# The first blocks redone: x and weights on one load queue in order of use, their four layer norms in a fixed order, transposes in half banks

## The chip, the cores and the metric

The kernel runs on one core of one Trainium2 chip. The metric is the device time of one execution in microseconds (us), lower is better. The kernel before took 1696.49 us, the median of 3 runs (1696.45 to 1697.39). Every run quoted here was in the fast state (the granted clock of the TensorE over the whole span was 0.998 to 1.0) and gave a correct result.

## The reference, cut to what matters

Four layers work on a 2048 x 1024 activation `x`. A linear attention block and a gated feed-forward block alternate, each behind a layer norm. Only the first attention block matters here, and of it only the start: normalise `x`, multiply by the key columns of `wqkv`, apply `phi`.

```python
def _layernorm(x, axis=-1, eps=1e-5):
    m = jnp.mean(x, axis=axis, keepdims=True)
    v = jnp.var(x, axis=axis, keepdims=True)
    return (x - m) / jnp.sqrt(v + eps)
# attention: S = 2048, D = 1024, 32 heads
    qkv = (x @ wqkv)...                       # cut: reshape into heads
    phi = lambda t: jnp.where(t > 0, t + 1, jnp.exp(t)) + 1e-6
    pq, pk = phi(q), phi(k)
    kv = jnp.einsum("bhsd,bhse->bhde", pk, v)
    # ... cut: num / den, @ wo
x = x + attention(_layernorm(x), wqkv, wo)
x = x + feed_forward(_layernorm(x), W_gate, W_up, W_down)
# ... and both once more
```

## The kernel before

`x` is cut into 16 blocks of 128 rows, x0 to x15. For each block VectorE takes statistics of its two halves (`bn_stats`), ScalarE makes the reciprocal deviation, VectorE scales, the matrix engine (PE) transposes eight 128x128 tiles into PSUM, and VectorE or ScalarE copies them back. Four blocks make one 512-column operand. With it PE computes k0 (the first half of the keys), then k1, v0 and v1. GpSimd (POOL) casts each block into the resident float32 copy of `x`. The parts that the change touches:

```python
        ident_f = self.xnp.tile([P, P], F32, tag="xn")
        make_identity(nc, ident_f[:, :])                      # GpSimd, float32
        self.ident = self.const.tile([P, P], BF16, name="ident")
        nc.vector.tensor_copy(out=self.ident, in_=ident_f)    # VectorE cast
# ... cut
    def ln_norm(self, layer, t):
        src = self.xin.pop(t) if layer == 0 else self.x[t]
        # ... cut: bn_stats of 2 halves, bn_aggr, Ln and Exp on ScalarE -> rstd
        nc.vector.tensor_scalar(out=xn, in0=src, scalar1=mv[:, 0:1], scalar2=rstd[:, 0:1],
                                op0=ALU.subtract, op1=ALU.mult)
        if layer == 0:
            nc.gpsimd.tensor_copy(out=self.x[t], in_=src)
            if t + 3 < self.ST:
                self.load_x(t + 3)
        return xn

    def ln_turn(self, layer, t, xn):
        # ... cut
        tp = self.pst.tile([P, self.KT, P], BF16, tag="tr")   # one PSUM buffer
        for kt in range(self.KT):
            nc.tensor.transpose(tp[:, kt, :], xn[:, kt * P:(kt + 1) * P], self.ident)
        # ... cut: one copy of the whole tile, VectorE and ScalarE in turn

    def load_x(self, t):
        xin = self.xio.tile([P, self.D], BF16, tag="xio")     # three buffers
        self.nc.scalar.dma_start(out=xin, in_=self.x_v[:, t, :])
        self.xin[t] = xin
# ... cut: layer_A
        ring.free_before((l, "k0"))       # seven weight tiles of 1 MB, on nc.sync
        for q in range(self.NQ):
            if l == 0 and q == 0:
                for j in range(QT):
                    self.ln_turn(l, j, self.ln_norm(l, j))
            if q + 1 < self.NQ:
                self.ln_later(l, q + 1, 2, 4, 2)
# ... cut: run
        for t in range(3):
            self.load_x(t)
        self.layer_A(0, 1)
```

There are three buffers for arriving blocks, so x3 is asked for only when x0 has been scaled and cast. And the scheduler of the kernel language decides, when the program is built and from its own estimates of times, in which order each engine gets its instructions. On the chip every engine then follows that order.

## Time and profile before

| | before |
|---|---|
| median of runs | 1696.49 us |
| span of the profiled run | 1694.7 us |
| PE busy | 1675.2 us, 99% of the span |
| first transposes start | 11.58 us |
| fifth block's transposes end, next matmuls start | 25.81 us |
| PE busy in the 25.81 us before that | 11.51 us |

From the page of the kernel before: the span, the busy times, and the chain of waits by engine.

```profile
span 1694.7 us, 19592 instructions
...
PE 1675.2 (99%) x8304; PEld 778.6 (46%) x8304; DVE 595.0 (35%) x1002; ACT 392.5 (23%) x723; POOL 21.2 (1%) x54
...
PE 95%; DVE 3%; ACT 1%; DMA 1%; issue 0%; DVEq 0%; ACTq 0%
```

The table of windows of the kernel before follows. The columns are the window, its length, then busy time and number of instructions for each engine, the granted PE clock, the DMA share and GB/s.

```profile
core 0: us, PE busy (x) PEld busy (x) DVE busy (x) ACT busy (x) POOL busy (x), PEclk, DMA share, GB/s
0.00:25.81 25.81, 11.51 (x73) 6.53 (x74) 15.24 (x37) 7.79 (x19) 7.53 (x20) 1.00 1.00 327
25.81:50.00 24.19, 24.19 (x151) 12.52 (x149) 17.62 (x37) 11.25 (x27) 6.60 (x9) 1.00 0.28 86
50.00:1691.00 1641.00, 1639.07 (x8085) 759.58 (x8084) 561.41 (x927) 373.49 (x679) 7.11 (x25) 1.00 0.36 117
```

PE is idle for 14.3 us in the first window (25.81 − 11.51), for nothing in the second, and for under 2 us in the other 1641 us. A change to the first blocks can earn something only in the first window, and what it earns there it keeps, because everything later is bound by PE.

The timeline of PE in the kernel before is next: start, duration, engine, line, operation, output<-inputs, count, and in brackets the idle time in front and what ended it. `tp` are transposes, `ps` matmuls.

```profile
11.58 1.01 PE L153 MATMUL tp<-ident,xn 128*128 128x128 bf16 x8 [11.58 <-DVE ident L109]
13.38 1.01 PE L153 MATMUL tp<-ident,xn 128*128 128x128 bf16 x8 [0.78 <-DVE xnT L157]
14.19 2.74 PE L229 MATMUL ps<-t,xnT 128*128 128x512 bf16 x6
16.75 0.62 PE L153 MATMUL tp<-ident,xn 128*128 128x128 bf16 x8
...
20.60 0.61 PE L153 MATMUL tp<-ident,xn 128*128 128x128 bf16 x8 [1.94 <-DVE xnT L157]
21.04 4.48 PE L229 MATMUL ps<-t,xnT 128*128 128x512 bf16 x20
25.36 0.61 PE L153 MATMUL tp<-ident,xn 128*128 128x128 bf16 x8
```

Three causes of the slow head show here. PE cannot start before 11.58 us. It waits again before 13.38 and 20.60 for copies of transposed blocks. And its first six matmuls are 427 ns apart (2.74 us for six, with the pipeline's end counted in), where the 20 at 21.04 are 216 ns apart. Below, the clock of PE is called closed, or cold, while matmuls run at this half rate, and open afterwards. At the later rate the five blocks and the 32 matmuls ahead of 25.81 need 32 x 0.216 + 5 x 0.44 = 9.1 us.

The timeline of VectorE in the kernel before, the same columns, cut to the steps that feed PE:

```profile
4.61 1.29 DVE L130 BATCH_NORM_STATS2 stats<-xin 128x6 f32<-128x512 bf16 x2 [3.09 <-DMA xin<-in_A_x_dram]
7.68 0.69 DVE L130 BATCH_NORM_STATS2 stats<-xin 128x6 f32<-128x512 bf16 x1 [1.78 <-DMA xin<-in_A_x_dram]
8.29 0.19 DVE L132 BATCH_NORM_AGGREGATE mv<-stats 128x2 f32<-128x12 f32 x1
...
9.08 1.06 DVE L137 TENSOR_SCALAR xn<-xin,mv,rstd 128x1024 bf16<-128x1024 bf16 x1
...
11.32 0.20 DVE L109 CAST ident<-ident_f 128x128 bf16<-128x128 f32 x1
...
16.54 1.29 DVE L130 BATCH_NORM_STATS2 stats<-xin 128x6 f32<-128x512 bf16 x2 [2.75 <-DMA xin<-in_A_x_dram]
...
19.40 0.55 DVE L137 TENSOR_SCALAR xn<-xin,mv,rstd 128x1024 bf16<-128x1024 bf16 x1
```

x0's statistics are taken at 4.61, as soon as x0 lands. But the built order puts a statistic of x1 in front of x0's aggregate, and x1 lands at 7.68. So x0 is scaled only at 9.08. The cast of the identity, which the first transpose needs too, comes at 11.32. x3 was asked for at 10.68 us, once x0's buffer was free, and VectorE waits 2.75 us for it at 16.54.

### The profile page before, as it was taken

The numbers are of one execution on the slowest core, as the hardware profiler recorded it, in microseconds if no ns is written. First come the engines' busy times: TensorE is split into PE (matmuls) and PEld (weight loads), VectorE is DVE, ScalarE is ACT, GpSimd is POOL, SyncE is SP. The second block draws the span as 40 slices with busy tenths as digits, with TensorE's granted clock in tenths as the row PEclk, the third lists the DMA queues.
The fourth block names the chain that finished last, engine by engine and source line by source line (L and its number), as shares of the span: only waits on it lengthen the run. The fifth ranks groups of instructions, "written<-read, shape, count | busy, mean of one in ns | idle before, by whom it ended". The sixth has DMA issues, their size and how long they took to land.

```text
span 1694.7 us, 19592 instructions
## 1 busy us (share of the span) xinstructions
PE 1675.2 (99%) x8304; PEld 778.6 (46%) x8304; DVE 595.0 (35%) x1002; ACT 392.5 (23%) x723; POOL 21.2 (1%) x54
## 2 busy tenths in 40 slices
PE   6999999999999999999999999999999999999999
PEld 3554444444444444444455544444444444444444
DVE  7445994312321231232144279832112202211211
ACT  3436641210220120022033374412002101100110
POOL 3100000000000000000000000000000000000000
PEclk9999999999999999999999999999999999999999
DMA  7103011455445444444510220134554464455441
GB/s 242 32 26 125 0 51 52 145 157 169 149 134 164 151 142 156 149 149 134 182 58 1 71 80 1 50 100 140 165 182 145 130 196 135 140 180 177 146 144 34
DMA packets 198489, 202.60 MB, mean 120 GB/s; under 512 B 3840, under 2 KB 196352, under 8 KB 198400
## 3 DMA queue, kind: packets, MB, share of 16 engines
q1 hardware_dynamic: 191488, 192.95, 35.4%
q10 hardware_dynamic: 6912, 8.39, 1.5%
q8 instruction: 65, 1.06, 0.3%
q14 instruction: 24, 0.20, 0.0%
HBM read 197.13 MB, written 4.19 MB: 119 GB/s over the span
## 4 chain that ended last, share of the span: by engine, by line
PE 95%; DVE 3%; ACT 1%; DMA 1%; issue 0%; DVEq 0%; ACTq 0%
PE acc L380 23%; PE pg L363 23%; PE pu L363 23%; PE ps L229 13%; PE ps L298 5%; PE ps L311 5%; PE tp L153 2%; PE kv L204 1%; PE ps L269 1%; DMA xin<-in_A_x_dram 1%; DVE stats L130 1%; DVE x L315 0%; DVE xn L137 0%; DVE pq L273 0%; ACT r L271 0%
## 5 line engine op out<-in xcount | busy, mean ns | idle before, releaser
L363 PEld LDWEIGHTS <-t 128*128 128x128 bf16 x3584 | 349.5, 98 | 416.3
L363 PE MATMUL pg<-xnT,t 128*128 128x512 bf16 x1792 | 423.3, 379 | 0.0
L363 PE MATMUL pu<-xnT,t 128*128 128x512 bf16 x1792 | 423.3, 379 | 0.0
L380 PE MATMUL acc<-t,hT 128*128 128x512 bf16 x1792 | 388.1, 379 | 0.0
L369 DVE TENSOR_TENSOR hT<-pu,rg 128x512 bf16<-128x512 f32 x224 | 154.9, 692 | 586.0 <-PE pu L363 586.0
L368 ACT ACTIVATE rg<-pg 128x512 f32<-128x512 f32 x224 | 133.3, 595 | 891.5 <-PE pg L363 891.4
L380 PEld LDWEIGHTS <-hT 128*128 128x128 bf16 x1792 | 175.3, 98 | 211.4
L229 PE MATMUL ps<-t,xnT 128*128 128x512 bf16 x1024 | 230.4, 380 | 0.0
L229 PEld LDWEIGHTS <-xnT 128*128 128x128 bf16 x1024 | 98.5, 98 | 109.9 <-issue 1.1
L298 PE MATMUL ps<-xnT,t 128*128 128x512 bf16 x512 | 121.6, 379 | 0.2
L311 PE MATMUL ps<-T,pq 128*128 128x512 bf16 x512 | 113.4, 379 | 0.0
L174 ACT ACTIVATE e<-ps 128x512 f32<-128x512 f32 x128 | 76.2, 595 | 137.1 <-PE ps L229 116.4
L391 DVE TENSOR_TENSOR xo<-x,acc 128x512 bf16<-128x512 f32 x32 | 22.0, 688 | 171.1 <-PE acc L380 167.5
L388 DVE TENSOR_TENSOR x<-x,acc 128x512 f32<-128x512 f32 x32 | 22.0, 688 | 159.4 <-PE acc L380 157.9
L311 PEld LDWEIGHTS <-pq 128*128 128x128 bf16 x512 | 50.0, 98 | 58.5
L298 PEld LDWEIGHTS <-t 128*128 128x128 bf16 x512 | 49.7, 98 | 56.1 <-issue 1.7
L175 DVE TENSOR_SCALAR e<-e 128x512 f32<-128x512 f32 x128 | 54.9, 429 | 57.3 <-ACT e L174 56.3
L130 DVE BATCH_NORM_STATS2 stats<-x 128x6 f32<-128x512 f32 x96 | 65.4, 691 | 2.4
L153 PE MATMUL tp<-ident,xn 128*128 128x128 bf16 x512 | 39.8, 222 | 14.3 <-DVE ident L109 11.6
L235 ACT ACTIVATE pkv<-ps 128x512 bf16<-128x512 f32 x64 | 38.2, 597 | 66.2 <-PE ps L229 66.2
L153 PEld LDWEIGHTS <-xn 128*128 128x128 bf16 x512 | 34.7, 99 | 29.5 <-DVE xn L137 12.0
L315 DVE TENSOR_TENSOR x<-x,ps 128x512 f32<-128x512 f32 x64 | 43.2, 675 | 12.5 <-PE ps L311 12.0
(41 smaller groups left out, 517.8 us busy)
## 6 DMA issues: line engine op xcount, KB each, us to landing
t<-in_B_W_gate_dram SPq DMA_DIRECT2D x56, 1024.0 KB, 5.4
t<-in_B_W_up_dram SPq DMA_DIRECT2D x56, 1024.0 KB, 5.2
t<-in_B_W_down_dram SPq DMA_DIRECT2D x64, 896.0 KB, 5.8
t<-in_A_wqkv_dram SPq DMA_DIRECT2D x12, 1024.0 KB, 5.6
xin<-in_A_x_dram ACTq DMA_DIRECT2D x16, 256.0 KB, 3.6
t<-in_A_wo_dram SPq DMA_DIRECT2D x4, 1024.0 KB, 5.2
out_dram<-xo ACTq DMA_DIRECT2D x32, 128.0 KB, 3.0
```

What stands on the lines that cost most here:

```text
L130: nc.vector.bn_stats(out=stats[:, c, :], in_=src[:, c * fmax:(c + 1) * fmax])
L153: nc.tensor.transpose(tp[:, kt, :], xn[:, kt * P:(kt + 1) * P], self.ident)
L174: nc.scalar.activation(out=e, in_=ps, func=ACT.Exp)
L175: nc.vector.tensor_scalar(out=e, in0=e, scalar1=1.0, scalar2=1e-6, op0=ALU.min, op1=ALU.add)
L229: nc.tensor.matmul(ps, lhsT=self.xnT[l, q][:, kt, j * P:(j + 1) * P], rhs=w[:, kt, :], start=(kt == 0), stop=(kt == KT - 1))
L298: nc.tensor.matmul(ps, lhsT=w[:, kt, (g % 4) * P:(g % 4 + 1) * P], rhs=self.xnT[l, sc][:, kt, :], start=(kt == 0), stop=(kt == KT - 1))
L311: nc.tensor.matmul(ps, lhsT=pq[sc, g // 4][:, g % 4, j * P:(j + 1) * P], rhs=T[g // 2][:, g % 2, n2 * NW:(n2 + 1) * NW], start=(g == 0), s ...
L315: nc.vector.tensor_tensor(out=xs, in0=xs, in1=ps, op=ALU.add)
L363: nc.tensor.matmul(ps, lhsT=w[:, kt, fi * P:(fi + 1) * P], rhs=self.xnT[l, q][:, kt, :], start=(kt == 0), stop=(kt == KT - 1))
L368: nc.scalar.activation(out=rg, in_=pg, func=ACT.Relu)
L369: nc.vector.tensor_tensor(out=h[:, fi, :], in0=pu, in1=rg, op=ALU.mult)
L380: nc.tensor.matmul(acc[j], lhsT=hT[ft // 4][:, ft % 4, j * P:(j + 1) * P], rhs=wd[:, k, :], start=(ft == 0), stop=(ft == self.FT - 1))
```

## The change

The intent is to start PE earlier: bring x0 first, then the weights k0, then x1 to x3, and so on, each when it is needed, all on one queue; give x0 to x3 buffers of their own, so that x3 need not wait for x0's; fix the order of VectorE's and ScalarE's work for the first four blocks; split each block's transposes into two half banks, one copied by VectorE and one by ScalarE; make the identity in bf16 at once; and delay the casts of x0 to x3. The core of the diff:

```diff
-        ident_f = self.xnp.tile([P, P], F32, tag="xn")
-        make_identity(nc, ident_f[:, :])
         self.ident = self.const.tile([P, P], BF16, name="ident")
-        nc.vector.tensor_copy(out=self.ident, in_=ident_f)
+        make_identity(nc, self.ident[:, :])
 ... cut: ln_norm split into ln_stat (one half), ln_rstd and ln_scale
+    def head(self):
+        xh = [self.slab.tile([P, 2, self.D], BF16, tag="slab", name=f"xh{i}") for i in range(2)]
+        src = [xh[j // 2][:, j % 2, :] for j in range(QT)]
+        load = lambda j: nc.sync.dma_start(out=src[j], in_=self.x_v[:, j, :])
+        load(0)
+        self.ring.load_to(1)                  # k0
+        for j in range(1, QT):
+            load(j)
+        self.ring.load_to(2)                  # k1
+        for t in range(QT, QT + 3):
+            self.load_x(t)
+        self.ring.load_to(4)                  # v0, v1
 ... cut
+        def first_units(j, xn):
+            for h in range(2):
+                tp = self.ps3.tile([P, H, P], BF16, tag="b")
+                ... four transposes
+                if h == 0:
+                    nc.vector.tensor_copy(out=dst, in_=tp)
+                else:
+                    nc.scalar.activation(out=dst, in_=tp, func=ACT.Copy)
+
+        with tc.manual_schedule(engines={mybir.EngineType.DVE, mybir.EngineType.Activation}):
+            self.ln_stat(0, src[0], 0, stats[0])
+            self.ln_stat(0, src[0], 1, stats[0])
+            r = self.ln_rstd(stats[0])
+            for j in range(QT):
+                if j + 1 < QT:
+                    self.ln_stat(j + 1, src[j + 1], 0, stats[j + 1])
+                xn = self.ln_scale(src[j], *r)
+                if j + 1 < QT:
+                    self.ln_stat(j + 1, src[j + 1], 1, stats[j + 1])
+                    r = self.ln_rstd(stats[j + 1])
+                first_units(j, xn)
+        for j in range(QT):
+            self.later.at(6 + j, lambda j=j: nc.gpsimd.tensor_copy(out=self.x[j], in_=src[j]))
 ... cut
-        self.nc.scalar.dma_start(out=xin, in_=self.x_v[:, t, :])
+        self.nc.sync.dma_start(out=xin, in_=self.x_v[:, t, :])
 ... cut: layer_A calls head() for the first four blocks; the other weights are asked for later
```

More of the change, by code (lines that the diff above doesn't have):

```diff
@@ L120, in __init__, with ln_stat, ln_rstd @@
         self.xnT = {}
-    def ln_norm(self, layer, t):
-        nc, D = self.nc, self.D
-        src = self.xin.pop(t) if layer == 0 else self.x[t]
-        fmax = min(nc.vector.BN_STATS_FMAX, D)
-        nch = D // fmax
-        stats = self.small.tile([P, nch, nc.vector.BN_STATS_DIM], F32, tag="stats")
-        for c in range(nch):
-            nc.vector.bn_stats(out=stats[:, c, :], in_=src[:, c * fmax:(c + 1) * fmax])
+    def ln_stat(self, t, src, c, stats):
+        fmax = self.D // 2
+        self.nc.vector.bn_stats(out=stats[:, c, :], in_=src[:, c * fmax:(c + 1) * fmax])
+    def ln_rstd(self, stats):
+        nc = self.nc
         mv = self.small.tile([P, nc.vector.BN_AGGR_DIM], F32, tag="mv")
@@ L135, in ln_norm, with ln_scale @@
         nc.scalar.activation(out=rstd, in_=rstd, func=ACT.Exp, scale=-0.5)
-        xn = self.xnp.tile([P, D], BF16, tag="xn")
-        nc.vector.tensor_scalar(out=xn, in0=src, scalar1=mv[:, 0:1], scalar2=rstd[:, 0:1],
-                                op0=ALU.subtract, op1=ALU.mult)
+        return mv, rstd
+    def ln_scale(self, src, mv, rstd):
+        xn = self.xnp.tile([P, self.D], BF16, tag="xn")
+        self.nc.vector.tensor_scalar(out=xn, in0=src, scalar1=mv[:, 0:1], scalar2=rstd[:, 0:1],
+                                     op0=ALU.subtract, op1=ALU.mult)
+        return xn
+    def ln_norm(self, layer, t):
+        nc = self.nc
+        src = self.xin.pop(t) if layer == 0 else self.x[t]
+        stats = self.small.tile([P, 2, nc.vector.BN_STATS_DIM], F32, tag="stats")
+        for c in range(2):
+            self.ln_stat(t, src, c, stats)
+        xn = self.ln_scale(src, *self.ln_rstd(stats))
         if layer == 0:
@@ L143, in ln_norm @@
         return xn
+    def head(self):
+        nc, tc = self.nc, self.tc
+        xh = [self.slab.tile([P, 2, self.D], BF16, tag="slab", name=f"xh{i}") for i in range(2)]
[9 more added lines that the diff above has]
+        self.ring.load_to(4)
+        self.xnT[0, 0] = self.xnTp.tile([P, self.KT, QT * P], BF16, tag="xnT", name="xnT0_0")
+        stats = [self.small.tile([P, 2, nc.vector.BN_STATS_DIM], F32, tag="stats", name=f"st{j}")
+                 for j in range(QT)]
+        H = self.KT // 2
+        def first_units(j, xn):
+            for h in range(2):
+                tp = self.ps3.tile([P, H, P], BF16, tag="b")
+                for i in range(H):
+                    kt = h * H + i
+                    nc.tensor.transpose(tp[:, i, :], xn[:, kt * P:(kt + 1) * P], self.ident)
+                dst = self.xnT[0, 0][:, h * H:(h + 1) * H, j * P:(j + 1) * P]
+                if h == 0:
[16 more added lines that the diff above has]
+            self.later.at(6 + j, lambda j=j: nc.gpsimd.tensor_copy(out=self.x[j], in_=src[j]))
     def ln_turn(self, layer, t, xn):
@@ L209, in kv_step @@
             del pk[t], va[t]
-        ring.free_before((l, "k0"))
+        if l:
+            ring.free_before((l, "k0"))
         for q in range(self.NQ):
             if l == 0 and q == 0:
-                for j in range(QT):
-                    self.ln_turn(l, j, self.ln_norm(l, j))
+                self.head()
+            if l == 0 and q == 1:
+                ring.free_before((l, "k0"))
             if q + 1 < self.NQ:
@@ L399, in run @@
         nc.scalar.preload_act_table_set("natural_log_exp_and_others")
-        for t in range(3):
-            self.load_x(t)
         self.layer_A(0, 1)
```

## The prediction

> **What bounds the kernel now.** The matrix engine: 1675.2 us busy of a 1694.7 us span (page), 95% of the chain of waits. The table of windows shows PE busy 11.5 us in 0 to 25.8 us; in the other 1669 us it is idle about 5 us (key/value fold 1 us, tail 3.3 us). So only the head can give anything. By 25.8 us PE has done five blocks of transposes and 32 matmuls; then it never stops until 141 us. At the later rate (32 matmuls in 6.91 us, 0.44 us a block) that is 9.1 us of work: 16.7 us are waiting or cold clock.
>
> **Why the head is slow (timeline).** x0 lands at 4.6 us, x1 at 7.65, because three weight megabytes on the other queue share the 350 to 395 GB/s. x0's statistics end at 5.9, but VectorE's order puts x1's first statistic before x0's aggregate (8.29); x0's scaling (1.06 us, beside a POOL cast) ends at 10.1; the identity's cast stands behind more statistics, and the first transpose starts at 11.58. Whole-bank copies through one PSUM buffer (0.7 us VectorE, 1.0 ScalarE) stop PE (0.8, 1.9 us). x3, issued at 10.7, has its transposes at 20.6. The first six matmuls run 427 ns apart, later ones 216. The Trainium skill, "TensorE: Matmul & The Clock Gate" (Part 1), says that some 3.4 us of activity release a half-rate clock; the trace agrees on the factor two, though the clock view says 1.00.
>
> **What the change does.** It removes the identity's cast (0.2 us, but on the path) and queues x0, k0, x1 to x3, k1, x4 to x6, v0, v1 in that order. "DMA: Bandwidth & Descriptors" (Issuing engines are not separate DMA queues) says that two queues add no bandwidth; here 347 GB/s moves while mostly one queue works: no loss expected. Estimates at 370 GB/s from 2 us: x0 lands at 3.4, k0 6.3, x1 7.1, x2 7.8, x3 8.5, k1 11.3. PE's instructions are the same, and after the first 32 matmuls so is their built order.
>
> The catch: VectorE's new order has x1's first statistic before x0's scaling, so x0's early landing is wasted until x1 lands at 7.1. Then statistic 0.65, scaling 0.5 to 1.0 (casts still beside it): first transposes at 8.3 to 8.8. From there VectorE is nearly saturated: up to the scaling of x4 stand nine statistics (0.6), five scalings (0.46), four half copies (0.35), two phi pairs (0.95), four aggregates: 12 to 13 us. PE runs cold to about 13 us. The fifth block's transposes, which ended at 25.8, should end at 20.5 to 21.3; after that phi keeps ahead through four PSUM buffers.
>
> **Gain:** 25.8 − 20.9 = 4.9 us, all on the critical path, since everything later is PE-bound. 1696.5 − 4.9 = 1691.6 us; 8 in 10: 1689.6 to 1694.0. Faster by over 2%: 0.005; within 2%: 0.99; slower: 0.005.
>
> **Signs.** First transpose at 8.3 to 8.8, released by VectorE's scaling; x1's landing near 7.1 ends VectorE's long wait; x3 landed by 9; fifth block near 20.5; PE busy total changed under 2 us; no PE wait from 21 to 141 us; tail as before.
>
> **What would make it wrong.** x1 to x3 landing later behind k0: up to +2 us. The clock staying at half rate longer because PE pauses between blocks: +1.5. x7 to x15 stuck behind weights on the same queue: should be harmless, x7 being needed after 40 us. VectorE waiting less than I think: −1.5.

## The result, and the profile after

The changed kernel took 1692.53 us, the median of 4 runs (1692.49 to 1692.66), against 1696.82 (1696.45 to 1697.39, 4 runs) for the kernel before in the same rounds: 4.29 us less. The ratio is 0.9975, with a 95% interval of 0.9957 to 0.9992. A ratio here is the mean time of one kernel's fast runs over that of the other's of the same rounds, so it is not quite the ratio of the medians. The interval excludes 1. All outputs are right.

From the page of the kernel after:

```profile
span 1690.8 us, 19608 instructions
...
PE 1676.2 (99%) x8304; PEld 778.4 (46%) x8304; DVE 596.7 (35%) x1003; ACT 393.2 (23%) x725; POOL 21.3 (1%) x54
...
PE 94%; DVE 3%; ACT 1%; DMA 1%; issue 0%; SPq 0%; DVEq 0%
```

The table of windows of the kernel after follows, with the same columns. The windows are cut at the same pieces of work: the first ends where the fifth block's transposes end.

```profile
0.00:21.46 21.46, 12.30 (x73) 6.34 (x74) 15.50 (x38) 8.00 (x19) 8.70 (x21) 1.00 0.98 323
21.46:45.65 24.19, 23.96 (x149) 12.35 (x147) 18.84 (x38) 10.89 (x29) 5.43 (x8) 1.00 0.48 148
45.65:1686.65 1641.00, 1639.07 (x8085) 759.49 (x8083) 561.59 (x927) 374.26 (x679) 7.19 (x26) 1.00 0.37 117
```

The first window is 4.35 us shorter (25.81 to 21.46), although PE is busy in it 0.8 us longer. In the third, 1641 us of work shifted by 4.35 us, PE is busy for 1639.07 us in both kernels. In the second PE is idle for 0.23 us, where it was not before: one wait for ScalarE's copy of the values, at 45.09 us, in front of a key/value product. So the head gave 4.35, the second window took back 0.23, and the span of the profiled run shrank by 3.9. The remaining 0.2 us I have not traced. (The medians differ by 4.29 us; the two profiled runs by 3.9.)

The timeline of PE in the kernel after:

```profile
8.62 1.04 PE L177 MATMUL tp<-ident,xn 128*128 128x128 bf16 x8 [8.62 <-DVE xn L136]
9.75 1.46 PE L285 MATMUL ps<-t,xnT 128*128 128x512 bf16 x3
11.00 1.06 PE L177 MATMUL tp<-ident,xn 128*128 128x128 bf16 x8
11.85 2.67 PE L285 MATMUL ps<-t,xnT 128*128 128x512 bf16 x6
14.36 0.61 PE L177 MATMUL tp<-ident,xn 128*128 128x128 bf16 x8
...
17.28 0.62 PE L177 MATMUL tp<-ident,xn 128*128 128x128 bf16 x8 [0.37 <-DVE xn L136]
...
21.00 0.62 PE L207 MATMUL tp<-ident,xn 128*128 128x128 bf16 x8
```

PE starts 3.0 us earlier, and after that it waits only 0.37 us before the fifth block, where it waited 2.7 us before. The clock opens between: the transposes at 11.00 still take 0.85 us to the next matmul, those at 14.36 take 0.45, 5.7 us after PE's first instruction.

The timeline of VectorE in the kernel after, cut to the first statistics, all five scalings and the first `phi` step. Below it is the timeline of POOL in the same kernel, only the casts of blocks.

```profile
3.59 1.29 DVE L123 BATCH_NORM_STATS2 st<-xh 128x6 f32<-128x512 bf16 x2 [2.06 <-DMA xh<-in_A_x_dram]
...
7.21 0.69 DVE L123 BATCH_NORM_STATS2 st<-xh 128x6 f32<-128x512 bf16 x1 [2.10 <-DMA xh<-in_A_x_dram]
7.82 0.74 DVE L136 TENSOR_SCALAR xn<-xh,mv,rstd 128x1024 bf16<-128x1024 bf16 x1
...
10.21 0.63 DVE L136 TENSOR_SCALAR xn<-xh,mv,rstd 128x1024 bf16<-128x1024 bf16 x1
...
12.61 1.00 DVE L136 TENSOR_SCALAR xn<-xh,mv,rstd 128x1024 bf16<-128x1024 bf16 x1
...
14.86 0.91 DVE L229 TENSOR_SCALAR e<-e 128x512 f32<-128x512 f32 x1 [0.65 <-ACT e L228]
...
16.69 0.53 DVE L136 TENSOR_SCALAR xn<-xh,mv,rstd 128x1024 bf16<-128x1024 bf16 x1
...
20.39 0.55 DVE L136 TENSOR_SCALAR xn<-xin,mv,rstd 128x1024 bf16<-128x1024 bf16 x1
```

```profile
7.24 3.20 POOL L197 CAST x<-xh 128x1024 f32<-128x1024 bf16 x3 [2.59 <-DMA xh<-in_A_x_dram]
...
12.29 3.20 POOL L148 CAST x<-xin 128x1024 f32<-128x1024 bf16 x3 [1.20 <-DMA xin<-in_A_x_dram]
```

The transposes of x0, x1, x3 and x4 start within 0.2 us behind their scaling, so there VectorE sets the pace. Those of x2 do not: its scaling ended at 13.61, and PE, still at half rate, reached it at 14.36. VectorE works from 7.21 to 20.94 us with only 0.65 us idle. Its scaling of 128x1024 elements takes 0.53 to 0.55 us when POOL casts nothing, and 0.74, 0.63 and 1.00 us while POOL's casts of 7.24 and 12.29 run. The `phi` step of 14.86, usually 0.42 us, took 0.91. The change meant to delay the casts of x0 to x3, but in the trace they run as soon as the blocks have landed: POOL has nothing else to do, and the delay only moved them in the program's order.

### The profile page after: what moved, and what is told of

It is laid out like the page before. It is cut to its first block, busy times and chain, and to the rows that moved or that the text cites. A ratio compares the mean times of both kernels' runs of the same rounds, so it can differ in the third digit from the quotient of the medians.

```text
span 1690.8 us, 19608 instructions
## 1 busy us (share of the span) xinstructions
PE 1676.2 (99%) x8304; PEld 778.4 (46%) x8304; DVE 596.7 (35%) x1003; ACT 393.2 (23%) x725; POOL 21.3 (1%) x54
## 3 DMA queue, kind: packets, MB, share of 16 engines
q8 instruction: 65, 1.06, 0.3%
## 4 chain that ended last, share of the span: by engine, by line
PE 94%; DVE 3%; ACT 1%; DMA 1%; issue 0%; SPq 0%; DVEq 0%
PE acc L436 23%; PE pu L419 23%; PE pg L419 23%; PE ps L285 12%; PE ps L354 5%; PE ps L367 5%; PE tp L207 1%; DVE stats L123 1%; PE kv L258 1%; PE ps L325 1%; DVE xn L136 1%; DVE x L371 0%; DVE e L229 0%; DVE pq L329 0%; DMA xh<-in_A_x_dram 0%
## 5 line engine op out<-in xcount | busy, mean ns | idle before, releaser
L130 ACT ACTIVATE rstd<-mv,eps 128x1 f32<-128x1 f32 x64 | 18.9, 295 | 121.7 <-DVE mv L128 121.7
L329 DVE TENSOR_TENSOR pq<-pq,r 128x512 bf16<-128x512 bf16 x64 | 43.8, 689 | 6.1 <-ACT r L328 3.7
```

The costliest lines, as they stand in the source:

```text
L329: nc.vector.tensor_tensor(out=p, in0=p, in1=r, op=ALU.mult)
```

## The experiments

The change has several parts, and the gain of 4.3 us is their sum. Each run below had 5 rounds, beside the kernel before on the same chip (medians 1696.54, 1696.42 and 1696.60). The kernel after was not run again in these rounds. It was run at another time. The quoted expectations call theories by letters. The ones that return most often are A, that the blocks' early landing gives the gain and VectorE then bounds the head; B, that the single queue in order of use is what gives it; F, that the closed clock holds the head; G, that early blocks and a fixed order are needed together; and I, that POOL's casts stretch VectorE's work.

One sum orders all the results. The sixth block's transposes are the first point where every variant has the same 64 matmuls behind it, so its start (call it T6) compares the heads. To it comes the longest PE wait for the key/value products between 38 and 46 us ("kv wait"), and in two variants the matmuls that ran at half rate after that wait ("cold"). The column "sum" is 1690.8 + (T6 − 28.36) + (kv wait − 0.23) + cold, all relative to the kernel after:

| kernel | median us (range) | ratio to before [95%] | T6 us | kv wait us | cold us | sum us | span profiled us |
|---|---|---|---|---|---|---|---|
| before | 1696.82 (1696.45–1697.39) | 1 | 32.71 | 0 | | 1694.9 | 1694.7 |
| after | 1692.53 (1692.49–1692.66) | 0.9975 [0.9957, 0.9992] | 28.36 | 0.23 | | 1690.8 | 1690.8 |
| a_two_queues | 1692.52 (1692.08–1693.42) | 0.9976 [0.9964, 0.9989] | 28.72 | 0 | | 1690.9 | 1690.7 |
| a_free_order | 1691.80 (1691.07–1691.86) | 0.9970 [0.9958, 0.9983] | 27.95 | 0 | | 1690.2 | 1690.0 |
| a_whole_banks | 1692.43 (1691.47–1692.66) | 0.9974 [0.9961, 0.9986] | 28.82 | 0 | | 1691.0 | 1690.8 |
| b_loads | 1693.35 (1693.14–1694.52) | 0.9983 [0.9969, 0.9997] | 29.10 | 0 | | 1691.3 | 1691.3 |
| b_buffers | 1697.39 (1696.71–1698.12) | 1.0005 [0.9992, 1.0017] | 34.00 | 0 | | 1696.2 | 1696.3 |
| a_scale_first | 1691.90 (1691.65–1692.77) | 0.9973 [0.9960, 0.9985] | 28.29 | 0.54 | | 1691.0 | 1691.0 |
| a_x1_first | 1693.86 (1693.73–1694.94) | 0.9986 [0.9973, 0.9998] | 30.50 | 0.50 | | 1693.2 | 1693.2 |
| a_warm | 1690.90 (1690.74–1691.61) | 0.9967 [0.9954, 0.9981] | 26.43 | 0.52 | | 1689.2 | 1689.1 |
| d_order_3bufs | 1694.91 (1694.56–1695.25) | 0.9987 [0.9974, 0.9999] | 30.26 | 0.31 | | 1692.8 | 1692.8 |
| a_casts_late | 1692.72 (1692.18–1693.48) | 0.9975 [0.9961, 0.9989] | 26.65 | 1.48 | | 1690.3 | 1690.3 |
| c_three | 1694.32 (1693.21–1695.14) | 0.9983 [0.9970, 0.9995] | 24.85 | 3.73 | 2.7 | 1693.5 | 1693.3 |
| c_four | 1695.09 (1694.10–1695.84) | 0.9987 [0.9975, 1.0000] | 24.22 | 4.83 | 2.9 | 1694.2 | 1694.1 |

The sum agrees with the span of each profiled run within 0.25 us. So the difference between any two of these profiled executions lies in the head, in one wait 40 us in, and in what that wait does to the clock. A profile is one execution, and not always a typical one: in b_buffers, a_scale_first, a_x1_first, c_three and c_four it is the slowest of the five runs, in b_loads, d_order_3bufs and a_casts_late the fastest. T6 also contains the moment at which the clock first opened, which no edit but the 60 matmuls of a_warm, c_three and c_four set on purpose. Full rate came by 16.8 us in before, 14.4 in after, 11.9 in a_casts_late and 21.5 in b_buffers. The runs of one kernel lie up to 2 us apart, so differences of half a microsecond between medians are near the limit of what these rounds can tell.

### a_two_queues: the changed kernel, its loads on two queues

```diff
-        load = lambda j: nc.sync.dma_start(out=src[j], in_=self.x_v[:, j, :])
-        load(0)
-        self.ring.load_to(1)
-        for j in range(1, QT):
+        load = lambda j: nc.scalar.dma_start(out=src[j], in_=self.x_v[:, j, :])
+        self.ring.load_to(7)
+        for j in range(QT):
             load(j)
 ... and load_x on nc.scalar again
```

> The changed kernel with the queues of before: all x blocks on the second queue, the seven weights on the first, everything asked for at once. The built order on PE, VectorE and ScalarE is that of the changed kernel. Theory A (VectorE, in order, is saturated from the landing of x1 until the fifth block's scaling, so only x1's landing and the lateness of x3 and x4 count): x0 lands at about 4.6 us, x1 at about 7.7 as in before, x2 to x4 in time; VectorE starts its run 0.5 us later; 1692.8 to 1693.6 us. Rival B (the single queue in order of use is the source of the gain): 3 us or more of the 4.3 us are lost, 1695.5 us or more.

Measured: 1692.52 us, equal to the kernel after. x1 reached VectorE at 7.39 us instead of 7.21, the first transposes started at 8.72 instead of 8.62. The time is a little better than theory A expected. The queue and its order of use give nothing once the rest of the change is in place, so theory B falls. This is what the Trainium skill, "DMA: Bandwidth & Descriptors" (Issuing engines are not separate DMA queues), leads one to expect: transfers of all issuing engines end up on the same 16 DMA engines and interleave.

### a_free_order: the changed kernel, the scheduler orders the layer norms

```diff
-        with tc.manual_schedule(engines={mybir.EngineType.DVE, mybir.EngineType.Activation}):
+        if True:
```

> The changed kernel without the fixed order of VectorE and ScalarE; loads and half banks stay. The scheduler puts x0's scaling ahead of x1's first statistic by itself, and two statistics of x4 and x5 ahead of x3's scaling. Theory A: within 1 us of the changed kernel either way, 1691.5 to 1693.5 us, first transposes near 6 us. Rival C (the fixed order is the source of the gain): 1695.5 us or more.

Measured: 1691.80 us; all five runs lie below the four of the kernel after, by 0.7 us at the medians. Left alone, the scheduler put x0's scaling in front of x1's statistic by itself, and the first transposes started at 6.34. With these loads the fixed order is no source of gain, and it seems to cost a little.

### a_whole_banks: the changed kernel, transposes copied as whole banks

```diff
-            for h in range(2):
-                tp = self.ps3.tile([P, H, P], BF16, tag="b")
 ... 
+            tp = self.pst.tile([P, self.KT, P], BF16, tag="tr")
+            for kt in range(self.KT):
+                nc.tensor.transpose(tp[:, kt, :], xn[:, kt * P:(kt + 1) * P], self.ident)
 ... one copy, VectorE for even blocks, ScalarE for odd ones
```

> The changed kernel with whole-bank transposes through the one buffer, copied by VectorE and ScalarE in turn as before. VectorE's work for copies is about the same (two of 0.6 against four of 0.35 us), PE gains waits for the one buffer. Theory A: 1692.8 to 1694.0 us. Rival D (half banks are the source of the gain): 1695.5 us or more.

Measured: 1692.43 us. The trace shows a PE wait of 0.79 us for the first copy and T6 0.46 us later, but the kv wait of 0.23 us is gone, and the times of the two kernels cannot be told apart. Half banks are worth at most some tenths of a microsecond here.

### b_loads: the kernel before, with the loads of the change only

```diff
+                xh = [self.slab.tile([P, 2, D], BF16, tag="slab", name=f"xh{i}") for i in range(2)]
+                for j in range(QT):
+                    self.xin[j] = xh[j // 2][:, j % 2, :]
+                    nc.sync.dma_start(out=self.xin[j], in_=self.x_v[:, j, :])
+                    if j == 0:
+                        ring.load_to(1)
+                ring.load_to(2)
+                for t in range(QT, QT + 3):
+                    self.load_x(t)
+                ring.load_to(4)
 ... and load_x on nc.sync
```

> The kernel before with the loads of the changed one alone: one queue in order of use, x0 to x3 in buffers of their own, x4 to x6 asked for at the start. Scheduler's order, whole banks and the identity's cast stay. Theory A: the late landings of x3 (16.5 us) and x4 (18.0 us), which came from three x buffers and not from the queue, go away; most of the gain is there: 1692.5 to 1694.0 us. Rivals C and D: less than a third of the gain, 1695.4 us or more.

Measured: 1693.35 us, 3.2 of the 4.3 us. From the timeline of VectorE in b_loads:

```profile
5.74 0.55 DVE L138 TENSOR_SCALAR xn<-xh,mv,rstd 128x1024 bf16<-128x1024 bf16 x1 [0.60 <-ACT rstd L136]
```

With these loads the scheduler itself put x0's scaling in front of x1's statistics, and it ran at 5.74, where the kernel before had it at 9.08. The first transposes then started at 9.44, and what released them was the cast of the identity (0.93 us long here, beside a POOL cast). The loads, with no other part of the change, bring three quarters of the gain.

### b_buffers: the kernel before, early blocks in buffers of their own, still on two queues

```diff
+                xh = [self.slab.tile([P, 2, D], BF16, tag="slab", name=f"xh{i}") for i in range(2)]
+                for j in range(QT):
+                    self.xin[j] = xh[j // 2][:, j % 2, :]
+                    nc.scalar.dma_start(out=self.xin[j], in_=self.x_v[:, j, :])
+                for t in range(QT, QT + 3):
+                    self.load_x(t)
```

> The kernel before with one thing changed: x0 to x3 in buffers of their own, and x4 to x6 asked for at the start too. Both queues, seven weights at once, scheduler's order, whole banks and the identity's cast are those of before. Theory A (the three x buffers, which made x3 and x4 be asked for only at 10.7 and 12.3 us, were the cause): x3 and x4 land by about 12 us instead of 16.5 and 18.0, and half or more of the gain is there, 1693.2 to 1694.6 us. Rival B (the order of the one queue was what helped in the run with the loads alone): 1695.5 us or more.

Measured: 1697.39 us, no gain at all. Theory A, as I had it, falls. All four blocks had landed by about 11 us. From the timeline of VectorE in b_buffers:

```profile
7.57 0.69 DVE L131 BATCH_NORM_STATS2 stats<-xh 128x6 f32<-128x512 bf16 x1 [1.27 <-DMA xh<-in_A_x_dram]
...
11.02 2.66 DVE L138 TENSOR_SCALAR xn<-xh,mv,rstd 128x1024 bf16<-128x1024 bf16 x2
```

What failed first is the built order. The scheduler placed x1's and x2's statistics in front of x0's scaling. The scalings of x0 and x1 came together at 11.02 and took 2.66 us, beside casts. PE started at 12.57, later than before, and the clock opened late too: the five matmuls at 19.38 were still 414 ns apart, and full rate came at 21.45, where the kernel before had it at 16.75. How much of the lost gain is the order and how much the clock, no run separates. So the landing times alone were not enough; that b_loads owed its gain in good part to the order that the scheduler built for it is the likely reading, which the next run tests from the other side.

### d_order_3bufs: the changed kernel, with the three old buffers and two queues

```diff
-        xh = [self.slab.tile([P, 2, self.D], BF16, tag="slab", name=f"xh{i}") for i in range(2)]
-        src = [xh[j // 2][:, j % 2, :] for j in range(QT)]
 ... 
+        self.ring.load_to(7)
+        for t in range(3):
             self.load_x(t)
+        src = [self.xin[t] for t in range(3)]
 ... 
                 xn = self.ln_scale(src[j], *r)
+                nc.gpsimd.tensor_copy(out=self.x[j], in_=src[j])
+                self.load_x(j + 3)
 ... and load_x on nc.scalar again
```

> The cell that is missing: the fixed order, half banks and direct identity of the changed kernel, but the loads of before: three x buffers, x3 asked for only when x0 is scaled and cast, two queues, seven weights at once. Theory G (the gain needs both, blocks that are there and an order of VectorE that does not wait for what is not there; either alone gives nothing or little): x3 is asked for at about 9 us and lands at about 14.5, VectorE waits 2 to 3 us for it at x3's first statistic, x4 lands near 16.5; 1694.5 to 1696 us. Rival H (the order alone gives the gain, since the run with early blocks and the scheduler's order gave nothing): 1693 us or less.

Measured: 1694.91 us, 1.7 of the 4.3 us. From the timeline of VectorE in d_order_3bufs:

```profile
14.77 0.69 DVE L123 BATCH_NORM_STATS2 st<-xin 128x6 f32<-128x512 bf16 x1 [2.10 <-DMA xin<-in_A_x_dram]
```

The order is now good, and the start is as in the kernel after (first transposes at 8.76), but x3 is missing: VectorE waits 2.10 us for it, and PE 1.42 and 0.91 us for VectorE. The four runs on two queues make a square:

| two queues | three x buffers | x0 to x3 in buffers of their own |
|---|---|---|
| scheduler's order | 1696.6 (before) | 1697.4 (b_buffers) |
| fixed order (and half banks, bf16 identity) | 1694.9 (d_order_3bufs) | 1692.5 (a_two_queues) |

Early blocks alone give nothing, the order (on two queues always together with the half banks and the bf16 identity) gives 1.7 us, and both together 4.0 us, each against before in its own rounds. Theory G fits: neither is enough without the other here. b_loads is a second way to both: with all loads on one queue in order of use the scheduler built a good order itself.

### a_scale_first: the changed kernel, x0's scaling in front of x1's statistic

```diff
-                if j + 1 < QT:
+                if 0 < j and j + 1 < QT:
                     self.ln_stat(j + 1, src[j + 1], 0, stats[j + 1])
                 xn = self.ln_scale(src[j], *r)
+                if j == 0:
+                    self.ln_stat(1, src[1], 0, stats[1])
```

> The changed kernel with x0's scaling ahead of x1's first statistic on VectorE; the rest of the order is the same. First transposes at 6.3 us instead of 8.6. Theory A: VectorE is still saturated from x1's landing at 7.2 us, so the gain is no more than the scaling that moved ahead of that, 0.5 to 0.9 us: 1691.6 to 1692.1 us. Rival E (the first transposes' start is what counts): 2 us gained, 1690.6 us or less.

Measured: 1691.90 us. PE started at 6.25 instead of 8.62, but T6 moved by 0.07 us only. VectorE still waits for x1 (0.96 us at 7.15), and two later scalings (1.09 and 1.32 us) and a `phi` step (1.24 us) fell beside casts. The median is 0.6 us below that of the kernel after and inside theory A's range. But the profiled run is the slowest of the five and shows none of it, and its clock opened later (its transposes at 14.02 still took 0.86 us to the next matmul); the other four lie below every run of the kernel after. So a gain of some 0.6 us is possible and not shown. The 2 us of rival E are ruled out: an earlier first transpose does not by itself bring its 2.4 us.

### a_x1_first: the changed kernel, x1 asked for in front of k0

```diff
         load(0)
+        load(1)
         self.ring.load_to(1)
-        for j in range(1, QT):
+        for j in range(2, QT):
```

> The changed kernel with x1 asked for before k0; nothing else moves in the built order. x1 lands at about 4.4 us, k0 at about 7.1, x2 and x3 as they were. Theory A: VectorE starts its run at 4.9 us and waits for k0's first matmuls and x2 only a little: it is 1.2 to 2 us ahead; the fifth block's transposes near 19.3 us; 1690.5 to 1691.4 us. If PE's cold clock and not VectorE bounds the head (rival F): the gain is under 0.7 us.

Measured: 1693.86 us, slower than the kernel after by 1.3 us. From the timeline of PE in a_x1_first, and from its table of windows:

```profile
10.85 1.44 PE L286 MATMUL ps<-t,xnT 128*128 128x512 bf16 x3 [3.54 <-DMA t<-in_A_wqkv_dram]
```

```profile
3.50:8.00 4.50, 1.03 (x8) 0.87 (x9) 3.70 (x8) 1.38 (x5) 2.02 (x2) 1.00 0.89 264
```

This profile is of the slowest of the five runs (1694.94 us), but the fastest (1693.73) is slower than the kernel after too. The first matmuls now wait 3.54 us for k0, which came at 10.85. 256 KB more in front of it, at the 377 GB/s that the kernel after moved between 3.5 and 8 us, are an estimated 0.7 us. But the rate fell too, to 264 GB/s between 3.5 and 8 us. Why it fell no run here shows. c_four below asks for x1 early on another queue, and its matmuls start at 8.40.

### a_warm: the changed kernel, 60 small matmuls first

```diff
+        wu = self.ps.tile([P, NW], F32, tag="a", name="warm")
+        for i in range(60):
+            nc.tensor.matmul(wu[:, 0:P], lhsT=self.ident, rhs=self.ident, start=True, stop=True)
```

> The changed kernel with 60 matmuls of the identity on PE from about 1.4 us on, whose result nobody reads. They run before PE has other work and end before 8 us. The matmuls from 9.7 us on then run 216 ns apart and not 427. Theory A (VectorE saturated): PE's faster start saves only the 0.65 us for which VectorE waited for the first matmul group, 1691.8 to 1692.5 us. Rival F (the cold clock bounds the head): 2.5 us gained, 1690.0 to 1690.6 us.

Measured: 1690.90 us, the fastest kernel of all: 5.5 us below the kernel before and 1.6 below the kernel after, and no run of it overlaps theirs. From the timeline of PE in a_warm:

```profile
1.35 5.65 PE L170 MATMUL warm<-ident 128*128 128x128 bf16 x60 [1.35 <-POOL ident masks.py:199]
...
9.67 1.25 PE L288 MATMUL ps<-t,xnT 128*128 128x512 bf16 x5 [0.51 <-DVE xnT L183]
```

These matmuls use no data but the identity, which is ready at 1.35 us. They keep PE busy until 7.0 us, and the first five real matmuls at 9.67 are through in 1.15 us (the next transposes start at 10.82), 230 ns each, where the first ones of the kernel after are 418 ns apart. T6 comes 1.93 us earlier. This agrees with the Trainium skill, "TensorE: Matmul & The Clock Gate" (Part 1), by which the clock starts at half rate and opens after about 3.4 us of activity; here full rate came at 5.9 us, 4.5 us after the first of the 60. The pause of 1.54 us before 8.55 did not close it. VectorE had no wait from 7.14 to 20.1 us in this run, and still the head got shorter. The fifth block came only 0.84 us earlier (20.16), because VectorE sets when it can come. But PE had 37 matmuls behind it by then instead of 32, and that is another 5 x 0.216 = 1.08 us. So neither A (VectorE alone is the bound) nor F (the clock alone) holds by itself.

### a_casts_late: the changed kernel, POOL's casts held back behind the first blocks

```diff
+            def cast():
+                if t < 7:
+                    nc.vector.tensor_copy(out=self.x[t][:, 0:1], in_=self.xnT[0, 1][:, 7, 0:1])
+                nc.gpsimd.tensor_copy(out=self.x[t], in_=src)
+                if t + 3 < self.ST:
+                    self.load_x(t + 3)
 ... cut: for t < 7 cast() is put off by later.at(6, cast); the column write reads the eighth block's xnT
 ... cut: the same column write in front of the casts of x0 to x3, which move from later.at(6 + j) to (10 + j)
```

> The changed kernel with POOL's casts of x0 to x6 held back until the fifth block has left PE (a one-column copy by VectorE, which the cast overwrites, makes them wait). VectorE's and PE's built order up to the fifth block is the same. Theory I (casts running beside VectorE stretch its scalings and its first phi step, the term that the prediction left out): the scalings take 0.53 us where they took 0.74, 0.63 and 1.00, the first phi step 0.42 where it took 0.91; 1.0 to 1.4 us gained, 1691.0 to 1691.6 us. If the stretching comes from something else: no change, 1692.3 to 1692.7 us.

Measured: 1692.72 us, not to be told apart from the kernel after, so theory I's time was missed, and the rival's range met within 0.02 us. The traces tell more. From the timeline of VectorE in a_casts_late, and then from that of PE:

```profile
12.40 0.53 DVE L136 TENSOR_SCALAR xn<-xh,mv,rstd 128x1024 bf16<-128x1024 bf16 x1
...
13.63 0.43 DVE L241 TENSOR_SCALAR e<-e 128x512 f32<-128x512 f32 x1
```

```profile
11.64 1.54 PE L297 MATMUL ps<-t,xnT 128*128 128x512 bf16 x6
```

Theory I holds for the head, but does not explain all of it. Every scaling now took 0.53 to 0.55 us and the `phi` step 0.43, which is 1.25 us less than in the kernel after, and T6 came 1.71 us earlier. The other half microsecond goes with the clock, which opened earlier in this run: the six matmuls at 11.64 took 1.38 us to the next transposes, where the six at 11.85 in the kernel after took 2.51, and VectorE's wait of 0.65 us for the first matmuls went away. Why the clock opened earlier no run shows. The gain was then given back: PE waited 1.48 us at 41.98 for values. The casts free the three buffers, so late casts mean late loads of x7 to x9, whose layer norms delay everything behind them in order. The casts thus sit between two costs: beside VectorE's scalings they stretch them, and behind they delay the loads.

### c_three and c_four: a_scale_first, a_warm and a_casts_late together; c_four with x1 on another queue as well

```diff
 c_three: the three edits above at once
 c_four, in addition:
         load(0)
+        nc.scalar.dma_start(out=src[1], in_=self.x_v[:, 1, :])
         self.ring.load_to(1)
-        for j in range(1, QT):
+        for j in range(2, QT):
```

> The changed kernel with three of the steps together: x0 scaled first, identity matmuls to open the clock, casts held back. Theory A with I (VectorE saturated from x1's landing at 7.2 us): its work until the fifth block's scaling falls from 13.0 us, as in the run with the open clock alone, by the scaling of x0 and the stretching, to about 11.3; fifth block's transposes at about 18.5 us instead of 21.0; 1689.8 to 1690.4 us. If the steps do not add: 1690.8 us or more.

> The same with x1 alone on the second queue, asked for at the start. x0 and k0 stay first on the first queue, so the fall of the transfer rate seen when x0 and x1 were both ahead of k0 on one queue should not come. x1 lands near 5 us; k0 near 7.2, x2 and x3 by 8.6. VectorE gets up to 2 us ahead; then PE's 8.7 us of work after k0's landing is the floor: fifth block near 17 us; 1688.3 to 1689.6 us. If the rate falls here too: not faster than c_three.

Measured: 1694.32 and 1695.09 us. They have the shortest heads of all, with T6 3.5 and 4.1 us ahead of the kernel after, and are 1.8 and 2.6 us slower than it. From the timeline of PE in c_three:

```profile
40.23 0.59 PE L275 MATMUL kv<-pkv 128*128 128x129 bf16 x4 [3.73 <-ACT pkv L308]
40.62 3.62 PE L302 MATMUL ps<-t,xnT 128*128 128x512 bf16 x8
```

From the timeline of ScalarE in c_three:

```profile
39.16 0.29 ACT L130 ACTIVATE rstd<-mv,eps 128x1 f32<-128x1 f32 x1 [5.32 <-DVE mv L128]
...
39.60 0.58 ACT L308 ACTIVATE pkv<-ps 128x512 bf16<-128x512 f32 x1
```

From the table of windows of c_three:

```profile
40.20:45.00 4.80, 4.77 (x21) 2.53 (x21) 4.14 (x9) 1.37 (x5) 1.47 (x3) 0.50 0.21 55
```

PE arrives earlier, and the late casts make the later blocks land later: VectorE waited 3.38 us for one that it took up at 37.14. ScalarE then stood 5.32 us behind a block's statistics, and the copy of the values that PE needed stood behind it in ScalarE's order. PE waited 3.73 us, and that gap closed the clock again: the granted clock is 0.50 from 40.2 to 45 us, and eight matmuls took 3.62 us instead of 1.89. About 5.4 us at half rate cost 2.7 us, which is my estimate from the window above and the next one (4.8 x 0.5 + 5 x 0.06, with clock 0.94 from 45 to 50 us); in the same way 2.9 us for c_four, from clock 0.50 up to 44 us and 0.79 from 44 to 50. In a_casts_late the gap of 1.48 us left the clock open. Part 1 of the page named above puts the closing at some 3.4 us of idleness. c_four fits that (the granted clock fell at 39.7 us, 3.8 us after PE's last instruction), but in c_three it fell at 38.7 us, only 2.2 us after.

## Why the prediction was right

The time: 1692.5 us measured, 1691.6 predicted, inside the range of 1689.6 to 1694.0. Point by point:

- **PE bounds everything but the head.** Right. The long window has the same PE busy time, 1639.07 us, in both kernels, and of the head's 4.35 us 3.9 arrived in the span of the profiled run (4.29 between the medians).
- **First transposes at 8.3 to 8.8, released by VectorE's scaling; x1 near 7.1; x3 landed by 9.** Right: 8.62, 7.21, and the latest landing of the four blocks 5.8 us after issue, the last of them asked for at 2.7.
- **x0's early landing is wasted behind x1's statistic.** The wait is there (2.10 us at 7.21). But a_scale_first, which takes it away, moved T6 by only 0.07 us and the median by 0.6. The step cost little.
- **From there VectorE needs 12 to 13 us up to x4's scaling, and the fifth block ends at 20.5 to 21.3.** Measured 13.7 us and 21.46. This is the term that was mis-sized. The prediction allowed a stretched scaling for x0 alone ("0.5 to 1.0, casts still beside it") and took 0.46 us for each of the five otherwise. They took 0.74 + 0.63 + 1.00 + 0.53 + 0.55 = 3.45 us, 0.8 more than 5 x 0.53, and a `phi` step took 0.5 more. Late casts (a_casts_late) brought VectorE's stretch down to 12.0 us, from 7.20 to 19.24, and moved T6 by 1.71, of which about 1.25 us are the casts. So the predicted gain of 4.9 us was 4.35. That it came so near is partly luck. Counted from x1's landing at 7.1, 12 to 13 us and 0.44 for the transposes end at 19.5 to 20.5, before the range that the prediction states. It seems to count from the first transposes, as its "From there" says. But its nine statistics and five scalings begin with x1's first statistic and x0's scaling, which it had already spent before the first transposes. In the trace eight and four follow them, in 12.3 us (8.62 to 20.94). By the prediction's own sizes the pair is worth 1.06 us (0.6 + 0.46, my estimate), which made up for most of the 1.3 us of stretching.
- **PE cold until about 13 us.** Roughly right: the transposes at 14.36 are the first at full rate. What the prediction left out is that this was worth buying back: a_warm gained 1.6 us.
- **No PE wait between 21 and 141 us; the tail as before.** Nearly: one wait of 0.23 us at 45.09.
- **The reasons given for the slow head.** Here the prediction was right about the sum and wrong about two parts. Sharing bandwidth between two queues cost nothing (a_two_queues), and whole-bank copies cost nothing that could be measured (a_whole_banks). What counted was VectorE's order and the late x3, and they count together: neither alone brings more than 1.7 us on two queues. The moment at which the clock opened has a part in these numbers too, which only a_warm isolates. The identity's cast was on the path in b_loads (it released the first transposes at 9.44), but no run separates its share.

What stays open: why the transfer rate fell in a_x1_first; what sets the moment at which the clock first opens, and whether the spread between runs of one kernel comes from it; the last 0.2 us between the head's gain and the span's; and whether a warm clock with the casts of x0 to x3 alone held back would beat a_warm. That last kernel was not tried.

## What to carry to other kernels

When PE is busy for 99% of a span, look for the one stretch where it is not, and read from the timeline which engine's order holds it there: two loads that land early help nothing when the built order puts their work in front of the first block's. Compare variants at a point where all have done the same work, and add up what they lose after it, because the shortest heads here (c_three, c_four) lost more 40 us later than they had won. And give PE something to do while it waits for its first data: 60 small matmuls were worth more than a third of the whole change.

## What the Trainium skill lacked or had wrong

- "TensorE: Matmul & The Clock Gate", Part 4, says that in transpose mode the full clock does not engage, and gives about 275 ns for a transpose in a kernel. Here eight transposes and the step to the next matmul took 0.85 us with the clock closed (106 ns each; after, 11.00 to 11.85) and 0.45 us with it open (56 ns each; after, 14.36 to 14.81). They run at both rates. (These are steps from one to the next; single durations in the profile are 219 ns with the clock open.) Whether transposes alone would open the clock no run shows.
- "TensorE: Matmul & The Clock Gate", Part 1, fits in the two rates (427 and 216 ns between matmuls). It puts the opening at around 4 us of activity, give or take 0.5, and the closing at some 3.4 us of idleness; here both vary more. After the same 60 matmuls from 1.35 us on, full rate came 3.3 us after the first in c_three and 4.5 in a_warm; in the kernel after it came 5.7 us after PE's first instruction. In c_three the granted clock fell after 2.2 us of idleness; 1.48 us in a_casts_late left it open. The page warns that clock events in a trace can be unreliable. What it does not say is that the granted clock can read 1.00 at the start while the matmuls run at half rate (before, 14.19 us), and reads 0.50 after a later gap (c_three). The spacing of matmuls is the safer sign at the start.
- "SBUF — State Buffer" (Who interferes with whom) says that copies, casts and `tensor_scalar` in two-port modes contend with GpSimd for a shared port pair, and names an exclusive lock. The trace agrees: `tensor_scalar` of 128x1024 took 0.53 us alone and up to 1.34 us beside POOL's casts (a_two_queues), while the statistics stayed at 0.68. The page has factors for single pairs of instructions and no size for a mix like this; here it was about 1.3 us of 13.7.
- No page has the fall of the load rate to 264 GB/s (3.5 to 8 us, a_x1_first, where the kernel after had 377) when a second small block stood in front of the first weight tile on one queue.
